# One ring of 1 MB slots for all operands, and 32-column TensorE tiles, in a two-problem attention decode kernel

## The chip, the cores and the metric

The kernel runs on one core of a Trainium2 chip. The metric is the device time of the launch in microseconds (us), as the median of several runs. The other figure used here, the span, goes from the first to the last instruction of one profiled run; it is about 2 us shorter. Each profile is of one run.

In the lines of the profile, PE is TensorE and PEld its weight loads, DVE is VectorE, ACT is ScalarE, POOL is GpSimd, and SPq is the queue of SyncE, which issues the loads. L337 is line 337 of the kernel. An arrow in brackets names what ended the idle time before an instruction. The granted clock is the share of TensorE's full clock that the chip allowed.

## The reference

Two independent problems, A and B, each do one decode step of grouped attention: one query row, 32 query heads, 16 key heads, 128 numbers per head. A looks at the last 2048 positions of its cache only, B at all 8192. The two output rows are joined.

```python
q = (x @ wq).reshape(32 heads, 128)          # x: 576 numbers, wq: 576 x 4096
scores = q . k * 128**-0.5                   # two query heads share one key head
o = softmax(scores) . v
out = o.reshape(4096) @ wo                   # wo: 4096 x 576
# A: k, v = last 2048 of 8192 positions;  B: k, v = all 8192 positions
```

All data are bf16. Every byte of K, V, wq and wo is read once: 102.8 MB. There is little arithmetic per byte, so the question is how well the kernel keeps its reads going.

## The kernel before

K and V come in slabs of 512 KB (2048 positions of one head, 4 KB per partition) through a ring of 13 slabs. wq and wo have their own region, in chunks. Each K slab is transposed on TensorE into PSUM, copied back to SBUF by ScalarE (half) and VectorE (half), and multiplied with a query matrix that is zero outside the two columns of the head:

```python
def pe_T(pe, s):                       # 16 transposes of a 512 KB slab of K
    ...
    ins = pe.matmul(pk_bf[bank][...], lhsT=slabs[:, b, t, :], rhs=ident[:, :], is_transpose=True, ...)

def pe_S(pe, s):                       # scores: 128 weight columns, of which 32 are heads
    for jj in range(4):
        ins = pe.matmul(sacc[:, jj * 512:(jj + 1) * 512], lhsT=qtm[:, P, g, :],
                        rhs=ktb[:, j, jj * 512:(jj + 1) * 512], start=(g == 0), stop=(g == HKV - 1))

def pe_V(pe, vi):                      # V is the weights, two columns of probabilities move
    for t in range(NBLK):              # NBLK = 16
        ins = pe.matmul(dst, lhsT=slabs[:, b, t, :], rhs=ptsb[P][:, bb, 2 * g:2 * g + 2], ...)
```

The order is: q of A, K of A, q of B, all of K of B (V of A is put in between), then all of V of B. wo of B is loaded before the V stage and applied during and after it.

## Time and profile before

The time is 292.9 us (291.66 to 293.63, three runs).

| What | Value | Where it is read |
|---|---|---|
| Span of the profiled run | 291.6 us | page header |
| Read from memory | 102.76 MB, 352 GB/s on average | DMA part of the page |
| Rate when the queue is never starved | 408 GB/s | windows, 220 to 270 us |
| Bytes at that rate | 252 us | 102.76 MB / 408 GB/s |
| Difference to the span | about 40 us | |

The page of the kernel before, the part with 40 equal slices of 7.29 us: the busy tenths of TensorE, its granted clock in tenths, the DMA engines' busy share in tenths, and the rate.

```profile
PE   0569995699999979997999989996395447445565
PEclk9999999985999999999999999999555555555555
DMA  5999999999999999999799998999879999999940
GB/s 162 317 327 409 354 351 352 371 398 401 406 406 398 410 409 380 355 356 389 295 301 368 375 375 297 379 405 412 318 267 412 408 409 406 409 407 408 407 161 2
```

The DMA engines look busy in nearly all slices, but only in the last quarter does the rate stay near 408 (slices 9 to 15 come close, with 398 to 410). The same kernel by windows (busy us of each engine and, in brackets, instructions; then the granted clock, the DMA share and the rate):

```profile
0.00:23.00 23.00, 10.32 (x162) 9.25 (x163) 0.00 (x0) 1.49 (x2) 6.13 (x11) 1.00 0.88 275
23.00:110.00 87.00, 77.42 (x952) 58.28 (x952) 31.20 (x51) 39.23 (x39) 0.00 (x0) 0.94 1.04 389
110.00:200.00 90.00, 84.94 (x1084) 61.98 (x1081) 37.67 (x53) 50.17 (x51) 0.00 (x0) 1.00 0.98 358
...
210.00:220.00 10.00, 7.04 (x222) 6.65 (x222) 5.14 (x23) 0.00 (x0) 0.00 (x0) 0.50 0.69 257
220.00:270.00 50.00, 26.92 (x903) 25.73 (x904) 6.03 (x38) 0.00 (x0) 0.00 (x0) 0.50 1.03 408
...
280.00:291.60 11.60, 6.08 (x196) 5.63 (x195) 2.45 (x14) 0.00 (x0) 0.00 (x0) 0.50 0.05 16
```

Taking in each window its length times (1 - rate / 408), the start loses 7.5 us, 23 to 110 us 4 us, the K stage of B (110 to 200 us) 11 us, the change to the V stage 4 us, and the end 11 us. Those are about 38 of the 40 us.

Why the K stage is slow is seen on the timeline of TensorE: a slab costs 16 transposes and four score matmuls back to back, here 119.46 - 118.56 = 0.90 us and 120.32 - 119.46 = 0.86 us. The columns are start, duration, engine, line, operation, output and inputs, shapes and count.

```profile
118.56 1.06 PE L337 MATMUL pk<-ident,slabs 128*128 128x128 bf16 x16
119.46 1.03 PE L356 MATMUL sacc<-ktb,qtm 128*128 128x512 bf16 x4
120.32 0.54 PE L479 MATMUL pk<-ptsb,slabs 128*128 128x2 bf16 x16
...
278.84 0.43 PE L479 MATMUL pk<-ptsb,slabs 128*128 128x2 bf16 x11
282.17 0.19 PE L479 MATMUL pk<-ptsb,slabs 128*128 128x2 bf16 x2 [2.90 <-issue]
```

About 1.76 us for 512 KB is 298 GB/s. With one V slab of A (0.40 us) after three of K, 2 MB take an estimated 5.7 us, or 369 GB/s, near the 358 of the stage. The last two lines are from the end: "2.90 <-issue" is idle time in which TensorE waited for nothing that the profile shows. Such gaps come about every 256 instructions in the V stage. Nearly all bytes have landed by 280 us (the last piece at 282.6 us), and TensorE has work until 289 us.

### The profile page before, as it was taken

The numbers are of one execution on the slowest core, as the hardware profiler recorded it, in microseconds if no ns is written. First come the engines' busy times: TensorE is split into PE (matmuls) and PEld (weight loads), VectorE is DVE, ScalarE is ACT, GpSimd is POOL, SyncE is SP. The second block draws the span as 40 slices with busy tenths as digits, with TensorE's granted clock in tenths as the row PEclk, the third lists the DMA queues.
The fourth block names the chain that finished last, engine by engine and source line by source line (L and its number), as shares of the span: only waits on it lengthen the run. The fifth ranks groups of instructions, "written<-read, shape, count | busy, mean of one in ns | idle before, by whom it ended". The sixth has DMA issues, their size and how long they took to land.

```text
span 291.6 us, 8755 instructions
## 1 busy us (share of the span) xinstructions
PE 224.6 (77%) x3930; PEld 178.9 (61%) x3930; DVE 87.8 (30%) x199; ACT 93.3 (32%) x94; POOL 6.1 (2%) x11
## 2 busy tenths in 40 slices
PE   0569995699999979997999989996395447445565
PEld 0568763489667757775677767775285437445554
DVE  0003331150344363336333363344541111011112
ACT  2004552221655557554655556553000000000000
POOL 8000000000000000000000000000000000000000
PEclk9999999985999999999999999999555555555555
DMA  5999999999999999999799998999879999999940
GB/s 162 317 327 409 354 351 352 371 398 401 406 406 398 410 409 380 355 356 389 295 301 368 375 375 297 379 405 412 318 267 412 408 409 406 409 407 408 407 161 2
DMA packets 37480, 103.33 MB, mean 354 GB/s; under 512 B 4162, under 2 KB 12356, under 8 KB 37444
## 3 DMA queue, kind: packets, MB, share of 16 engines
q1 hardware_dynamic: 37444, 102.78, 94.1%
q8 instruction: 31, 0.51, 0.7%
q14 instruction: 5, 0.04, 0.0%
HBM read 102.76 MB, written 0.00 MB: 352 GB/s over the span
## 4 chain that ended last, share of the span: by engine, by line
PE 51%; SPq 14%; DMA 12%; issue 12%; DVE 6%; ACT 4%; DVEq 0%; ACTq 0%
PE sacc L356 17%; PE pk L337 17%; DMA slabs<-in_B_v_cache_dram 7%; SPq L232 7%; DMA slabs<-in_A_k_cache_dram 5%; SPq L273 4%; PE sacc L479 4%; PE pk L479 4%; PE pk L310 3%; DVE ssb L394 3%; PE pk L493 3%; ACT psb L405 2%; SPq L230 2%; PE sacc L493 2%; ACT ktb L375 1%
## 5 line engine op out<-in xcount | busy, mean ns | idle before, releaser
L375 ACT ACTIVATE ktb<-pk 128x1024 bf16<-128x1024 bf16 x80 | 81.6, 1022 | 99.8 <-PE pk L337 99.8
L337 PE MATMUL pk<-ident,slabs 128*128 128x128 bf16 x1280 | 87.6, 222 | 8.6 <-DMA slabs<-in_A_k_cache_dram 7.1
L337 PEld LDWEIGHTS pk<-ident,slabs 128*128 128x128 bf16 x1280 | 78.5, 99 | 24.8 <-DMA slabs<-in_A_k_cache_dram 8.6
L356 PE MATMUL sacc<-ktb,qtm 128*128 128x512 bf16 x320 | 82.7, 381 | 4.3 <-DVE stat L394 4.3
L377 DVE COPY ktb<-pk 128x1024 bf16<-128x1024 bf16 x80 | 55.3, 691 | 97.8 <-PE pk L337 97.8
L356 PEld LDWEIGHTS sacc<-ktb,qtm 128*128 128x128 bf16 x320 | 28.0, 98 | 24.4 <-issue 5.3
L479 PE MATMUL sacc<-ptsb,slabs 128*128 128x2 bf16 x672 | 23.4, 165 | 13.0 <-issue 7.2
L310 PE MATMUL pk<-xsb,wreg 128*128 128x1 bf16 (+1 forms) x320 | 20.2, 172 | 12.7 <-DMA wreg<-in_A_wq_dram 12.7
L479 PEld LDWEIGHTS sacc<-ptsb,slabs 128*128 128x128 bf16 x672 | 21.0, 104 | 14.1 <-issue 8.5
L310 PEld LDWEIGHTS pk<-xsb,wreg 128*128 128x128 bf16 (+1 forms) x320 | 18.1, 104 | 14.9 <-issue 8.2
L479 PEld LDWEIGHTS pk<-ptsb,slabs 128*128 128x128 bf16 x608 | 20.0, 101 | 11.6 <-issue 5.4
L479 PE MATMUL pk<-ptsb,slabs 128*128 128x2 bf16 x608 | 21.4, 164 | 7.4 <-issue 5.2
L493 PE MATMUL pk<-ostage,wreg 128*128 128x1 bf16 x192 | 11.3, 165 | 5.7 <-issue 5.7
L493 PE MATMUL sacc<-ostage,wreg 128*128 128x1 bf16 x128 | 10.6, 165 | 5.7 <-issue 5.7
L493 PEld LDWEIGHTS pk<-ostage,wreg 128*128 128x128 bf16 x192 | 9.3, 104 | 8.8 <-issue 8.8
L394 DVE CUSTOM_DVE_ANT_0 ssb<-sacc,zrow 32x2048 bf16<-32x2048 f32 x5 | 11.4, 2279 | 1.8 <-PE sacc L356 1.8
L405 ACT ACTIVATE psb<-ssb,stat 32x2048 bf16<-32x2048 bf16 x5 | 9.9, 1988 | 3.8 <-DVE stat L399 3.8
L556 DVE CAST ostage<-sacc 128x2 bf16<-128x2 f32 x21 | 3.3, 159 | 25.8 <-PE sacc L479 25.8
L493 PEld LDWEIGHTS sacc<-ostage,wreg 128*128 128x128 bf16 x128 | 8.4, 104 | 2.9 <-issue 2.9
L323 DVE CAST qtm<-pk 128x32 bf16<-128x32 f32 x2 | 0.4, 192 | 30.3 <-PE pk L310 30.3
L556 DVE CAST ostage<-pk 128x2 bf16<-128x2 f32 x11 | 1.8, 159 | 14.7 <-PE pk L479 14.7
L493 PE MATMUL pk<-otsb,wreg 128*128 128x1 bf16 x128 | 4.2, 164 | 2.5 <-DVE stat L394 2.5
(49 smaller groups left out, 63.7 us busy)
## 6 DMA issues: line engine op xcount, KB each, us to landing
slabs<-in_B_k_cache_dram SPq DMA_DIRECT2D x64, 512.0 KB, 6.5
slabs<-in_B_v_cache_dram SPq DMA_DIRECT2D x64, 512.0 KB, 11.5
slabs<-in_A_k_cache_dram SPq DMA_DIRECT2D x16, 512.0 KB, 14.4
slabs<-in_A_v_cache_dram SPq DMA_DIRECT2D x16, 512.0 KB, 6.0
wreg<-in_A_wo_dram SPq DMA_DIRECT2D x4, 1152.0 KB, 12.9
wreg<-in_B_wo_dram SPq DMA_DIRECT2D x4, 1152.0 KB, 11.6
wreg<-in_A_wq_dram SPq DMA_DIRECT2D x4, 1024.0 KB, 8.7
wreg<-in_B_wq_dram SPq DMA_DIRECT2D x4, 1024.0 KB, 14.6
```

Source lines behind the costliest of these rows:

```text
L230: sp.dma_start(wqv[:, 0:4, cols], wq[0:512, cols].rearrange("(k p) n -> p k n", p=128)).then_inc(s_wq[P][c], 16)
L232: sp.dma_start(wqv[0:DM - 512, 4, cols], wq[512:DM, cols]).then_inc(s_wq[P][c], 16)
L273: sp.dma_start(slabs[:, b, :, :].rearrange("p t d -> p (t d)"), src).then_inc(s_slab_full[b], 16)
L310: ins = pe.matmul(pk[3][:, P * HQ + h:P * HQ + h + 1], lhsT=wqv[0:rows, kt, h * DH:(h + 1) * DH], rhs=xsb[0:rows, P, kt:kt + 1], start=(kt ...
L337: ins = pe.matmul(pk_bf[bank][:, (t - 8 * half) * 128:(t - 8 * half + 1) * 128], lhsT=slabs[:, b, t, :], rhs=ident[:, :], start=True, stop ...
L356: ins = pe.matmul(sacc[:, jj * 512:(jj + 1) * 512], lhsT=qtm[:, P, g, :], rhs=ktb[:, j, jj * 512:(jj + 1) * 512], start=(g == 0), stop=(g ...
L375: ins = eng.activation(dst, src, ACT.Copy)
L377: ins = eng.tensor_copy(dst, src)
L394: dve.tensor_tensor_reduce(out=ssb[P][0:HQ, c4 * SLAB:(c4 + 1) * SLAB], in0=sacc[0:HQ, :], in1=zrow[0:HQ, :], scale=1.0, scalar=-1.0e30, o ...
L405: act.activation(psb[P][0:HQ, c4 * SLAB:(c4 + 1) * SLAB], ssb[P][0:HQ, c4 * SLAB:(c4 + 1) * SLAB], ACT.Exp, bias=st(P, C_NB + c4), scale=S ...
L479: ins = pe.matmul(dst, lhsT=slabs[:, b, t, :], rhs=ptsb[P][:, bb, 2 * g:2 * g + 2], start=(t == 0), stop=(t == NBLK - 1))
L493: ins = pe.matmul(outT[P][nt], lhsT=wov[:, h, c0:c0 + 128], rhs=col, start=first, stop=last)
```

## The change

It is a rewrite. Its intent: let nothing but the reads take time.

- All of wq, K, V and wo go through one ring of 12 slots of 1 MB, 8 KB per partition, in the order of use. A K slot holds 4096 positions of one head of B, or 2048 of two heads of A.
- The scores and V use four column tiles of 32. Each tile has its own 32 weight columns and its own 32 output partitions, and the four are meant to run side by side. For V the roles are swapped: the probabilities are the weights, V moves.
- The softmax has 128 rows (four tiles of 32 heads), so its VectorE and ScalarE instructions run over rows a quarter as long.
- K of a chunk alternates with V of the chunk before. wo of B is loaded last.

The core of the diff, with cuts (here and below `...` marks what is left out):

```diff
-SLAB = 2048
-NBUF = 13
+SLOT = 4096
+NSLOT = 12
...
-            ins = pe.matmul(sacc[:, jj * 512:(jj + 1) * 512],
-                            lhsT=qtm[:, P, g, :],
-                            rhs=ktb[:, j, jj * 512:(jj + 1) * 512],
-                            start=(g == 0), stop=(g == HKV - 1))
+                for h in range(CW[P] // 512):
+                    for j in range(4):
+                        o = e * CH[P] + j * CW[P] + h * 512
+                        ins = pe.matmul(sacc[32 * j:32 * j + 32, h * 512:(h + 1) * 512],
+                                        lhsT=qtm[:, P, g * 32:(g + 1) * 32], rhs=kt[:, u, o:o + 512],
+                                        start=(g == 0), stop=(g == HKV - 1))
...
-            ins = pe.matmul(dst,
-                            lhsT=slabs[:, b, t, :],
-                            rhs=ptsb[P][:, bb, 2 * g:2 * g + 2],
-                            start=(t == 0), stop=(t == NBLK - 1))
+                for b in range(CB[P]):
+                    for j in range(4):
+                        t = e * NT[P] + j * CB[P] + b
+                        o = (b * 4 + j) * 512 + 30 * g + 30
+                        ins = pe.matmul(opsum[32 * j:32 * j + 32, 0:DH], lhsT=ptm[:, pb, o:o + 32],
+                                        rhs=slots[:, s, t * 128:(t + 1) * 128], ...)
...
+    def load_wq(P, k):
+        rows = 128 if k < 4 else DM - 512
+        return load(lambda: wqs[P][k * 128:k * 128 + rows, :], lambda v: v[0:rows, :], "wq")
...
+    pb1 = k_phase(1, 1, between_b1)      # K of the second chunk of B, V of the first in between
+    v_some(1, 0, vb0, HKV)
...
+    v_some(1, 1, vb1, HKV)
+    combine(1)
+    for k in range(5):
+        wo_part(1, k, load_wo(1, k))     # wo of B: last
```

## The prediction

> **What bounds it now.** The page's header: span 291.6 us, 102.8 MB moved, mean 352 GB/s. In the stretches where the queue is never starved (228 to 270 us, table of windows) the 16 DMA engines deliver 407 to 409 GB/s at a DMA share above 1.0. At 408 GB/s the bytes alone take 252 us, so about 40 us of the span is DMA time not used. I read four places in the slices and windows:
> - 0 to 23 us: 195 to 320 GB/s, with 4162 packets under 512 B (x, element by element) and 2 KB rows of wq.
> - 110 to 200 us, the K stage of B: 298 to 409 GB/s, mean about 358. The chain of waits shows it PE-bound: 16 transposes 0.89 us and four 512-column score matmuls 0.88 us, 1.77 us per 512 KB (296 GB/s). DMA issue waits 74.6 us for K evictions.
> - 208 to 217 us: ring full until the first V of B (257 GB/s), PE clock 0.50.
> - 280 to 291.6 us: no DMA. PE finishes V and wo at clock 0.50, with 2.8 us "issue" gaps about every 256 instructions.
>
> **What the change does.** The same bytes, in 1 MB slots (12 of them, 30 us of transfers at 408 GB/s), with long rows. Transposes stay: 32 x 56 ns = 1.8 us per K slot. Scores are 8 matmuls per slot on four column tiles: 8 x 220 ns = 1.76 us serial, 0.44 if four run at once. The Trainium skill, "TensorE: Matmul & The Clock Gate", Part 3, measures 2.38x for three column tiles, so I take 0.6 us. V now moves 128 columns against 32-column weights: 32 x 56 ns, 1.8 us serial, about 0.6 in fours. So K costs about 2.4 us and V 0.6 against 2.57 us of DMA each. Evictions per K slot: ACT 2 x 1.02 = 2.04 us, DVE 2 x 0.69 = 1.4; both fit. PE instructions fall from 7860 to about 6500 and spread evenly, so fetch gaps hide behind the ring. Added: the softmax weight chains (about 4 us of PE waiting each) and mode switches; 30 us of ring absorbs them. wo of B comes last, when V is done: only 16 small matmuls, one copy and the 1.5 us output write follow the last load.
>
> **Sum.** First bytes about 2 us; 102.8 MB at 408 GB/s 252; small dips (64-row wq slots, starts) 2; tail 4. That is 260 us, nearly all of it DMA. Even serial column tiles (K 3.6, V 1.8 us) would mostly hide: K plus V 5.4 us against 5.14.
>
> **Predicted: 260 us, 8 in 10 between 254 and 270.** Faster by over 2%: 0.96; within 2%: 0.03; slower: 0.01.
>
> **Signs.** DMA share of 9 in nearly all slices and 400 to 410 GB/s from about 3 us until 5 us before the end; chain of waits mostly DMA into slots; DMA issue waits on PE are just the ring's pace; score matmuls in fours, about 0.5 to 0.7 us per slot; last load to end under 5 us.
>
> **What would break it.** The PE clock. The half clock measured here doubles transposes (115 ns each at 23 us, before the clock rose). The same page, Part 4, says that transposes do not count as activity in the same way; scores, now four times shorter, may not hold the clock up. Then K takes about 4.7 us plus V 1.2, against 5.14: the ring runs dry of free slots in B's K stages, and the time goes to 275 to 285 us. Before, with idle gaps of 2.8 us between K slabs, the clock stayed at 1.0, so I give this one in ten. The other way: 8 KB rows could raise the rate to 415 GB/s, giving 255 us.

## The result

The time is 262.5 us (262.43 to 263.82, four runs) against 293.13 us for the kernel before. The ratio is 0.898, with a 95% interval of 0.895 to 0.901. Ratios here are worked out from the fast runs of both kernels, so they are not quite the ratio of the medians that are quoted.

The slices of the changed kernel (6.5 us each):

```profile
PE   0559995179899795778967649768665443443472
PEclk9999999658799799797999997797886755555555
DMA  7999999999999999999999999999999999999971
GB/s 263 420 328 409 409 417 419 233 421 414 418 414 410 421 413 414 416 420 416 424 420 419 419 420 421 419 420 420 421 422 415 425 421 419 422 417 421 423 325 55
```

TensorE is 66% busy, the DMA engines are busy from the first slice to the last but two, and the rate is 409 to 425 apart from the dips, mostly above 408. Two dips (slices 3 and 8) and the end stand out. By windows:

```profile
0.00:3.00 3.00, 0.00 (x0) 0.00 (x0) 0.00 (x0) 1.49 (x2) 2.24 (x14) 1.00 0.40 79
...
13.00:17.00 4.00, 1.97 (x16) 0.27 (x16) 0.00 (x0) 0.00 (x0) 4.00 (x3) 1.00 0.96 274
...
46.00:52.00 6.00, 1.05 (x8) 0.14 (x8) 0.00 (x0) 0.00 (x0) 0.00 (x0) 0.59 0.99 224
...
60.00:110.00 50.00, 41.56 (x753) 33.15 (x751) 19.99 (x36) 25.34 (x27) 0.00 (x0) 0.89 1.02 415
110.00:200.00 90.00, 64.94 (x1292) 52.28 (x1289) 31.28 (x53) 38.03 (x41) 0.00 (x0) 0.89 1.01 420
200.00:240.00 40.00, 18.36 (x548) 14.16 (x548) 0.76 (x4) 0.00 (x0) 0.00 (x0) 0.54 1.01 420
...
250.00:257.50 7.50, 3.96 (x116) 3.10 (x118) 0.05 (x1) 0.00 (x0) 0.00 (x0) 0.50 0.48 196
257.50:260.60 3.10, 0.65 (x16) 0.35 (x16) 0.31 (x1) 0.00 (x0) 0.00 (x0) 0.50 0.00 0
```

At 420 GB/s the bytes take 244.7 us. With the same sum as above, the start loses 2.4 us, the dips 1.4 and 2.8 us, 250 to 257.5 us 4.0 us, and the end without reads 3.1 us. The stage from 110 to 200 us, which had lost 11 us, loses nothing: TensorE is busy for 65 of 90 us and waits for data. The timeline of TensorE:

```profile
42.18 0.40 PE L298 MATMUL opsum<-slots,xpad 128*32 128x512 bf16 x4 [0.91 <-DVE xpad L285]
42.40 0.40 PE L298 MATMUL misc<-slots,xpad 128*32 128x512 bf16 x4
42.61 0.40 PE L298 MATMUL opsum<-slots,xpad 128*32 128x512 bf16 x4
...
54.93 6.47 PE L335 MATMUL ktps<-ident,slots 128*128 128x128 bf16 x64
61.33 0.62 PE L356 MATMUL sacc<-kt,qtm 128*32 128x512 bf16 x8
...
161.35 1.96 PE L335 MATMUL ktps<-ident,slots 128*128 128x128 bf16 x32 [0.51 <-DMA slots<-in_B_k_cache_dram]
163.24 0.61 PE L356 MATMUL sacc<-kt,qtm 128*32 128x512 bf16 x8
163.84 0.63 PE L448 MATMUL opsum<-slots,ptm 128*32 128x128 bf16 x32
```

Four matmuls of 512 columns on four tiles start every 0.22 us (42.18, 42.40, 42.61), which is what one such matmul took before (0.88 us for four). So the four tiles do run side by side. Between transposes, eight take about 0.55 to 0.6 us instead of 1.76; why the gain is smaller there was not tested. The Trainium skill ("TensorE: Matmul & The Clock Gate", Part 3) has 2.38 times for three column tiles; this trace shows 4 times for four in an unbroken stream and about 3 times in the K slots.

The end, on the timeline of all engines: the last load releases 16 small matmuls, a copy and the output write.

```profile
257.48 0.67 PE L483 MATMUL misc<-slots,opj 128*32 128x144 bf16 x16 [0.36 <-DMA slots<-in_B_wo_dram]
258.21 0.31 DVE L489 CAST outsb<-misc 128x144 bf16<-128x144 f32 x1 [8.15 <-PE misc L483]
258.54 0.64 SPq L494 DMA_DIRECT2D out_dram<-outsb  x1
```

### The profile page after: what moved, and what is told of

Read it like the earlier page. It is cut to its first block, busy times and chain, and to the rows that moved or that the text cites. A ratio compares the mean times of both kernels' runs of the same rounds, so it can differ in the third digit from the quotient of the medians.

```text
span 260.6 us, 7123 instructions
## 1 busy us (share of the span) xinstructions
PE 171.7 (66%) x3292; PEld 132.6 (51%) x3292; DVE 68.9 (26%) x126; ACT 85.2 (33%) x92; POOL 21.6 (8%) x31
## 2 busy tenths in 40 slices
DMA packets 16369, 103.22 MB, mean 396 GB/s; under 512 B 1618, under 2 KB 1620, under 8 KB 6996
## 3 DMA queue, kind: packets, MB, share of 16 engines
HBM read 102.76 MB, written 0.00 MB: 394 GB/s over the span
## 4 chain that ended last, share of the span: by engine, by line
DMA 56%; SPq 27%; PE 14%; issue 1%; DVE 1%; ACT 0%
SPq L244 27%; DMA slots<-in_B_v_cache_dram 21%; DMA slots<-in_B_k_cache_dram 10%; DMA slots<-in_B_wo_dram 10%; PE ktps L335 10%; DMA slots<-in_B_wq_dram 9%; DMA slots<-in_A_k_cache_dram 6%; PE sacc L356 2%; PE opsum L448 1%; PE misc L483 0%; DVE qrow L307 0%; PE opsum L298 0%; SPq L105 0%; PE misc L298 0%; DVE srow L411 0%
## 5 line engine op out<-in xcount | busy, mean ns | idle before, releaser
L335 PE MATMUL ktps<-ident,slots 128*128 128x128 bf16 x1280 | 94.0, 243 | 24.6 <-DMA slots<-in_B_k_cache_dram 24.2
L335 PEld LDWEIGHTS ktps<-ident,slots 128*128 128x128 bf16 x1280 | 87.6, 111 | 32.7 <-DMA slots<-in_B_k_cache_dram 28.4
L342 ACT ACTIVATE kt<-ktps 128x1024 bf16<-128x1024 bf16 x80 | 78.7, 1022 | 74.9 <-PE ktps L335 74.8
L345 DVE COPY kt<-ktps 128x1024 bf16<-128x1024 bf16 x80 | 55.4, 692 | 93.0 <-PE ktps L335 93.0
L448 PE MATMUL opsum<-slots,ptm 128*32 128x128 bf16 x1280 | 31.7, 256 | 26.6 <-DMA slots<-in_B_v_cache_dram 26.5
L448 PEld LDWEIGHTS opsum<-slots,ptm 128*32 128x32 bf16 x1280 | 24.5, 114 | 39.7 <-DMA slots<-in_B_v_cache_dram 35.1
L356 PE MATMUL sacc<-kt,qtm 128*32 128x512 bf16 x320 | 25.4, 395 | 0.7 <-DVE kt L345 0.7
L220 POOL MEMSET ptm<- 128x8192 uint32 x2 | 13.8, 6924 | 0.0
L483 PE MATMUL misc<-slots,opj 128*32 128x144 bf16 x256 | 8.4, 307 | 5.4 <-DMA slots<-in_B_wo_dram 3.3
L483 PEld LDWEIGHTS misc<-slots,opj 128*32 128x32 bf16 x256 | 6.6, 134 | 6.9 <-DMA slots<-in_B_wo_dram 4.2
```

The costliest lines, as they stand in the source:

```text
L220: add("pool", lambda pool, b=b: pool.memset(ptm[:, b, :].bitcast(U32), 0), writes=[("ptm", b)])
L335: ins = pe.matmul(ktps_bf[q][:, t * 128:(t + 1) * 128], lhsT=slots[:, s, (8 * q + t) * 128:(8 * q + t + 1) * 128], rhs=ident[:, :], start= ...
L342: add("act", lambda act, q=q, dst=dst: act.activation(dst, ktps_bf[q], ACT.Copy), reads=[("bank", q)], writes=[("kt", u, q)])
L345: add("dve", lambda dve, q=q, dst=dst: dve.tensor_copy(dst, ktps_bf[q]), reads=[("bank", q)], writes=[("kt", u, q)])
L356: ins = pe.matmul(sacc[32 * j:32 * j + 32, h * 512:(h + 1) * 512], lhsT=qtm[:, P, g * 32:(g + 1) * 32], rhs=kt[:, u, o:o + 512], start=(g ...
L448: ins = pe.matmul(opsum[32 * j:32 * j + 32, 0:DH], lhsT=ptm[:, pb, o:o + 32], rhs=slots[:, s, t * 128:(t + 1) * 128], start=(g == 0 and b ...
```

## The experiments

The theory: after the change the reads bound the kernel nearly everywhere, their rate is set by the row length, and TensorE has slack. The rivals are that the time still comes from how TensorE's work is arranged (side-by-side tiles, alternation, ring depth), and that the dips and the end have other causes. Eleven kernels ran, the kernel before beside them, and all gave correct results. The changed kernel itself ran before these. Differences to its 262.5 us therefore are good to 1 or 2 us, and smaller ones say nothing. Where the ratio to the kernel before gives another size, both are told.

### Undoing single parts: row length

```diff
-                return a[0, i, r0:r0 + n, :].rearrange("(p t) d -> p (t d)", p=128)
+                return a[0, i, r0:r0 + n, :].rearrange("(h p t) d -> p h (t d)", h=2, p=128)
```

> Changed kernel, with one edit: each 1 MB slot of K and V of B is read as 2 x 4 KB per partition instead of 8 KB; number of transfers, ring and engine work stay. Theory A (bytes per row set the rate; one 4 KB packet took 159 ns before, one of 8 KB takes 312 ns): the rate in the V stage falls from 420 to about 409 GB/s and the time rises by 4 to 5 us, to 267. Rival B (the rate rose because there are half as many transfers, or because the engines disturb memory less): rate 418 to 421 and time within 0.7 us of 262.5.

Measured: 267.62 us (266.95 to 267.74), ratio to before 0.908 (0.903 to 0.914). The window of the V stage, which showed 420 GB/s in the changed kernel, with rows of 4 KB:

```profile
200.00:240.00 40.00, 18.24 (x496) 13.78 (x500) 1.98 (x12) 0.30 (x1) 0.00 (x0) 0.50 1.02 409
```

The medians differ by 5.1 us, the ratios to the kernel before (0.908 and 0.898) by about 3 us, and the rate falls back to that of the kernel before. The 67.1 MB of K and V of B at 409 instead of 420 GB/s are an estimated 4.3 us. The number of transfers, the ring and the engines' work are the same. So rows of 8 KB instead of 4 KB give 420 instead of 408 to 409 GB/s, and theory A holds. In the trace a row of 4 KB takes 159 to 162 ns on its DMA engine, one of 8 KB 312 ns.

### Undoing single parts: the order of the tiles

```diff
-                for b in range(CB[P]):
-                    for j in range(4):
+                for j in range(4):
+                    for b in range(CB[P]):
```

(and the same turn of the two loops of the scores)

> Changed kernel, with the loops turned so that successive matmuls of the scores and of V use the same column tile (V: eight in a row), so that little runs side by side. Theory A (transfers bound the kernel; the column tiles only had to bring TensorE under the transfer time): V per slot rises from 0.45-0.6 to about 1.7 us and scores from 0.54 to about 1.1 us at full clock, the clock stays up more, TensorE waits less for DMA, and the time stays within 2 us of 262.5. Rival B (side-by-side tiles are what the time comes from): K plus V over 5 us, ring starved, time above 268 us.

Measured: 263.32 us (262.82 to 264.09), ratio 0.894 (0.889 to 0.900). V per slot, on the timeline of TensorE at full clock:

```profile
163.83 1.34 PE L448 MATMUL opsum<-slots,ptm 128*32 128x128 bf16 x32
```

V costs 1.34 us instead of 0.63; the scores did not get slower (0.62 us), perhaps because they have only two matmuls per tile. So the edit took less of the overlap away than expected, and on that point the expectation missed. Still, V at twice the cost left the time where it was: 0.8 us more by the medians, while the ratio of 0.894 is even below 0.898.

### Adding TensorE work

```diff
-                for t in range(8):
+                for t in list(range(8)) * 2:     # every transpose of K twice
```

> Changed kernel with every K transpose done twice (same result), about 1.8 us more of TensorE per K slot at full clock: K 4.3 us and V 0.6 instead of 2.5 and 0.6, near the 5.4 us per pair that the prediction gave for column tiles that do not overlap. Theory A (prediction: such an excess mostly hides behind the ring and the V slots): time at most 270 us. Rival B (without side-by-side tiles the K stages are bound by TensorE): stages of K alone and of 2 K to 1 V run at under 350 GB/s and the time is 275 us or more.

Measured: fast runs of 267.57 and 270.31 us; two more, 271.84 and 271.68, are marked slow as they lie over 1.5% above the fastest. Their clocks (0.94 and 0.92) are those of the fast runs (0.95 and 0.92), so this may be the kernel's own spread. The ratio of the fast runs is 0.916 (0.908 to 0.923). The window from 110 to 200 us:

```profile
110.00:200.00 90.00, 86.00 (x1787) 77.11 (x1785) 27.76 (x41) 38.70 (x39) 0.00 (x0) 1.00 0.99 402
```

With 64 transposes per slot (3.7 us), an estimated 40 x 1.8 = 72 us of TensorE work was added, and 5 to 8 us of it show in the fast runs. The rate was 413 GB/s from 20 to 43 us and 402 from 110 to 200 us; the lowest slice there has 313. The fast runs lie on both sides of the 270 us of theory A, the median of all four is 271.0, and none reaches the 275 us of the rival. TensorE thus has much slack, but not without limit. In the stage with one V to each K, a pair took 4.7 us of TensorE (153.33 to 158.01 us), still less than the 5.0 us of its two transfers.

### Undoing single parts: alternation and ring depth

```diff
-        if i >= 2:
-            v_some(1, 0, vb0, 1)          # e6: no V between the K slots of the last K stage
```

> Changed kernel without the alternation in the last K stage: all 16 K slots of B's second chunk, then all 16 V slots of its first. Theory A (a K slot alone costs TensorE 2.5 to 2.56 us against 2.5 us of transfer, and the ring takes up the rest): within 1 us of 262.5, TensorE 90% or more busy in that K stage. Rival B (alternation is needed to keep the queue fed): the rate falls clearly below 410 GB/s in that stage and the time rises by 3 us or more.

```diff
-NSLOT = 12
+NSLOT = 6                                 # e5
```

> Changed kernel with a ring of 6 slots (6 MB, 15 us of transfers) instead of 12; the kernel before had 6.5 MB. Theory A (TensorE keeps pace per slot, so the ring only has to cover short waits): within 1 us of 262.5. Rival B (the deep ring is what hides the softmax chains and cold stretches): DMA rate dips in B's K stages and the time rises by 4 us or more.

Measured: without alternation 263.2 us (262.73 to 264.36), with TensorE busy for 39.4 of the 42 us of that K stage and 420 GB/s. With 6 slots 263.76 us (262.84 to 264.48), 416 instead of 420 GB/s from 110 to 200 us, with two slices below 400 (387 and 392). The first agrees with its theory A. The second is 1.3 us slower by the medians, a little more than the 1 us that was allowed, and far from the 4 us of its rival; the ratios (0.897 and 0.899, against 0.898) show no difference for either. Neither alternation nor the depth of the ring explains the gain; once a K slot costs TensorE no more than its transfer takes, 6 MB of lookahead is nearly enough.

### Undoing single parts: what is loaded last

```diff
-    v_some(1, 1, vb1, HKV)
+    v_some(1, 1, vb1, HKV - 6)
+    wob = [load_wo(1, k) for k in range(5)]
+    v_some(1, 1, vb1, HKV)                # the last six V slots land after wo
     combine(1)
```

> Changed kernel, but wo of B is loaded ahead of the last six V slots, so that V lands last. Theory A (loading wo last hides the combination of V and the 128 wo matmuls under its own transfers): after the last load TensorE still has one V slot (1.0 us), the combination (about 3 us) and 128 wo matmuls (about 4 us at half clock), so the end comes about 7 us later: 268 to 270 us. Rival B (the order of the last loads does not matter, as the end is set by the slowest DMA engine): within 1 us of 262.5.

Measured: 269.71 us (269.17 to 270.64), ratio 0.916 (0.910 to 0.922). The timeline of the end:

```profile
256.61 1.04 PE L448 MATMUL opsum<-slots,ptm 128*32 128x128 bf16 x32 [1.41 <-DMA slots<-in_B_v_cache_dram]
...
258.57 1.92 PE L470 MATMUL misc<-acc,pick 128*128 128x32 f32 x8 [0.92 <-DVE acc L464]
...
260.86 4.03 PE L483 MATMUL misc<-slots,opj 128*32 128x144 bf16 x128 [0.38 <-DVE opj L474]
...
265.28 0.64 SPq L494 DMA_DIRECT2D out_dram<-outsb  x1
```

From the last load to the output write 8.7 us pass, against 1.1 us (257.48 to 258.54) in the changed kernel. The order of the last loads is worth 7 us (5 us by the ratios).

### One part of the change alone, on the kernel before

```diff
-            ins = pe.matmul(sacc[:, jj * 512:(jj + 1) * 512],
-                            lhsT=qtm[:, P, g, :],
+            ins = pe.matmul(sacc[32 * jj:32 * jj + 32, jj * 512:(jj + 1) * 512],
+                            lhsT=qtm[:, P, g, 0:32],
...
-        dve.tensor_tensor_reduce(...)      # copy of the scores and their maximum in one
+        # four copies of 512 columns to partitions 0 to 31, then tensor_reduce for the maximum
```

> The kernel before, with one part of the change alone: its score matmuls go to four column tiles of 32 (the maximum is then taken in a copy and a reduction). Theory A (B's K stage was bound by TensorE at 1.77 us per 512 KB, half of it scores): scores per slab fall from 0.88 to about 0.3 us, the stage runs at 400 GB/s or more instead of 358, and the time falls by 8 to 11 us, to 282 to 285. Rival B (the stage was bound by evictions or by the ring): within 2 us of before. Neither removes the V stage's end at half clock, so 270 or less would refute both.

Measured: 286.23 us (284.3 to 287.49) against 293.93, ratio 0.973 (0.968 to 0.979). The timeline of TensorE in the K stage, and then the window of the stage:

```profile
120.95 1.14 PE L337 MATMUL pk<-ident,slabs 128*128 128x128 bf16 x16
122.03 0.40 PE L356 MATMUL sacc<-ktb,qtm 128*32 128x512 bf16 x4
122.36 1.14 PE L337 MATMUL pk<-ident,slabs 128*128 128x128 bf16 x16
```

```profile
110.00:200.00 90.00, 77.04 (x1253) 57.76 (x1251) 47.54 (x70) 52.70 (x52) 0.00 (x0) 0.88 1.00 380
```

A slab now costs 122.36 - 120.95 = 1.41 us instead of 1.76: the scores take 0.33 us instead of 0.86, but the 16 transposes between them 1.08 instead of 0.90. The stage runs at 380 GB/s instead of 358, less than the 400 that was expected. The gain of 7.7 us is just under the lower end of theory A and refutes its rival. So the score tiles alone give about a quarter of the 31 us; the stage of the kernel before was bound by TensorE. What still held it below 400 was not tested. The trace shows three candidates: the slower transposes; at the end of each chunk the separate maximum (2.29 us), which stands in the chain of waits; and the clock, which averages 0.88 in the stage (1.00 before).

### The two dips

The dips coincide with the last slot of wq of A and of B: 64 rows, which went to 64 of the 128 partitions. The experiment sends these rows as 128 half rows. x then needs two columns for them, one with zeros in the odd places and one with zeros in the even places.

```diff
-        rows = 128 if k < 4 else DM - 512
-        return load(lambda: wqs[P][k * 128:k * 128 + rows, :], lambda v: v[0:rows, :], "wq")
+        if k < 4:
+            return load(lambda: wqs[P][k * 128:k * 128 + 128, :], lambda v: v, "wq")
+        return load(lambda: wqs[P][512:DM, :].rearrange("r (h n) -> (r h) n", h=2),
+                    lambda v: v[:, 0:2048], "wq")
...
+                    kk, o = (k, n * 512) if k < 4 else (4 + j // 2, (n % 4) * 512)
```

> Changed kernel, with one edit: the last 64 rows of wq go as 128 half rows to all 128 partitions instead of 64 whole rows to 64 partitions. Theory A (the two dips to 160-310 GB/s at 13-16 us and 46-52 us come from writing only half of the partitions): both dips go, about 1.4 + 2.8 us are gained, 258 to 259 us. Rival B (the dips come from something else at that time, such as the stalled TensorE, its low clock, or the GpSimd memsets): the dips stay and the time stays at 262.5 us within 0.5.

Measured: 258.44 us (258.38 to 258.50), ratio to before 0.877 (0.871 to 0.884). The same two windows as above:

```profile
13.00:17.00 4.00, 0.00 (x0) 0.00 (x0) 4.00 (x2) 0.00 (x0) 4.00 (x1) 1.00 1.03 419
46.00:52.00 6.00, 5.00 (x68) 2.76 (x68) 1.00 (x3) 1.01 (x2) 0.00 (x0) 0.72 1.02 426
```

Both dips are gone and 4.1 us are gained (6 us by the ratios), as theory A has it. The Trainium skill ("SBUF — State Buffer", Door 1: The DMA port swizzle) says that partitions 0 to 63 reach only half of the 16 DMA ports, with 196 GB/s measured for 1 MiB; in the dips of the changed kernel single microseconds show 160 to 307 GB/s and the longer dip 224 on average, which roughly agrees.

The 4.00 us of VectorE from 13 to 17 us in this kernel are no work: the copies of 64 numbers that spread x were issued while GpSimd cleared a large tile, and took 11.05 us instead of 0.18.

```profile
3.39 13.79 POOL L222 MEMSET ptm<- 128x8192 uint32 x2
...
7.09 11.09 DVE L283 COPY xz<-xrow 1x64 bf16<-1x64 bf16 x2 [7.09 <-DMA xrow<-in_A_x_dram]
```

It put TensorE's first matmul off from 7.4 to 18.3 us, and the rate did not suffer: twelve slots give 30 us. The same skill page (SBUF: two separate sides) calls the port pair that GpSimd and VectorE share an exclusive lock, which the one that starts first holds for its whole instruction. The trace agrees that the copy is blocked and not slowed in proportion, but the wait outlasted one instruction: the first clearing ended at 10.32 us, and the copies only at 18.14 and 18.17 us, after a second one and four short ones that followed it without a pause (to 18.08 us).

### The slow last stretch

From 250 to 257.5 us the rate falls although reads are still queued. The trace has 16 completions for each load, one for the part of each DMA engine (it does not name the engines). Here they are for the first, a middle and the last load of e1 (the middle one completed at about 102 us), in us after the earliest engine, and for the last load of the two kernels that follow (worked out from the trace, one number per engine, sorted):

```
e1, first load      0.0 0.1 0.1 0.2 0.3 0.3 0.3 0.3 0.4 0.4 0.4 0.4 0.5 0.5 0.6 0.6
e1, middle load     0.0 0.1 0.1 0.2 0.4 0.5 1.2 1.3 1.6 1.8 1.8 1.9 1.9 2.1 2.1 3.5
e1, last load       0.0 0.0 0.2 0.4 0.5 0.7 1.2 1.3 4.7 4.8 4.9 5.0 5.0 5.1 5.1 6.4
e9, last load       0.0 0.3 0.4 0.4 0.5 1.1 1.2 1.3 4.8 5.0 5.0 5.0 5.0 5.0 5.0 5.2
e8, last load       0.0 0.1 0.1 0.2 0.3 0.4 0.8 1.1 4.4 4.5 4.8 4.9 6.2 6.3 6.3 6.3
```

Eight engines fall behind in steps, mostly of 1.3 to 1.4 us, one engine per step, and do not catch up in the rest of the run. In the same trace there are 26 fetches of instructions of 16 KB, nearly all of 1.0 to 1.1 us on a DMA engine. TensorE has 6643 instructions there, which is 26 pieces of 256 (e9: 6387 and 25 fetches; e8: 8203 and 32). The steps follow the fetches: those at 29.7 and 36.6 us, for example, are followed by the first late engine in the load that completes from 31.8 us on, and a second in the one from 36.9 us. Two experiments on top of e1 change the number of fetches.

```diff
+            for _ in range(30 if (P, c) == (1, 1) else 0):      # and in each wo slot
+                pe.matmul(sacc[0:1, 0:1], lhsT=ident[:, 0:1], rhs=ident[:, 0:1], start=True, stop=True)
```

> The kernel of e1_wq128 plus 30 idle matmuls of one column in each of the last 26 slots: 780 matmuls, 1560 TensorE instructions, about 6 more instruction fetches of 16 KB. In the trace of e1 each fetch sets one of eight DMA engines back by 1.3 us, in turn, for good, and the last engine ends 6.4 us after the first. Theory A (these set-backs fix the end): 32 fetches, all eight at 5 to 6.5 us or more, and the time is within 1 us of 258.4 or up to 1.4 us longer, with the spread of the last load at 6.4 us or more and more engines in the late group. Rival B (the spread comes from something else): same number of late engines as in e1 (8, one of them at 6.4).

```diff
-OUTW = DM // 4
+OUTW = DM // 2
...
-                for j in range(4):
+                for j in range(2):
...
-                    ins = pe.matmul(misc[32 * j:32 * j + 32, 0:OUTW], lhsT=opj[:, P, jj:jj + 32],
+                    ins = pe.matmul(misc[64 * j:64 * j + 64, 0:OUTW], lhsT=opj[:, P, jj:jj + 64],
```

> The kernel of e1_wq128, and wo on two column tiles of 64 instead of four of 32: 128 matmuls and 256 TensorE instructions fewer, one fetch of 16 KB. Theory A (each fetch sets one of eight DMA engines back 1.3 us for good): the fetch that came at 246 us in e1 comes later or not at all before the loads end, the spread of the last load falls from 6.4 to about 5.1 us, 257 to 257.6 us. Rival B: no change of the spread, 258.4 us, or a little more for the longer end.

Measured for e9: 257.31 us (257.22 to 257.43), ratio to before 0.876 (0.872 to 0.880), spread of the last load 5.2 us instead of 6.4, as theory A has it. It is the fastest kernel. It ran in another call than e1, so the 1.1 us between them are not from one chip; the evidence is the spread.

Measured for e8: 270.06 us (269.82 to 270.26), a miss: 1.4 us at most were expected, and it took 11.6 us more than e1. The loads ended as early as in e1, with four engines at 6.2 to 6.3 us instead of one at 6.4, so on the spread theory A is borne out. But TensorE no longer kept up at half clock, because of gaps of the kind that the kernel before had in its V stage:

```profile
215.37 0.27 PE L459 MATMUL opsum<-slots,ptm 128*32 128x128 bf16 x1
218.31 0.58 PE L459 MATMUL opsum<-slots,ptm 128*32 128x128 bf16 x13 [2.67 <-issue]
...
253.84 0.40 PE L459 MATMUL opsum<-slots,ptm 128*32 128x128 bf16 x6 [0.77 <-issue]
```

With 124 instead of 64 instructions per V slot, 256 instructions pass in about 3.3 us, and then TensorE stands for 2.7 us, until the next piece is there: the fetch in this gap began at 215.8 us and took 1.0 us. The six long gaps of the kernel before likewise each hold the start of a fetch, at 247.9, 254.1, 260.4, 266.9, 273.4 and 279.6 us. When the loads are done, the gap shrinks: 0.77 us at 253.84 us in e8, 0.27 us at 285.93 us in the kernel before. So e8 produced the end of the kernel before on purpose, and few instructions per byte matter while the DMA engines are full.

A last attempt was to give the last load to eight engines only (the code is shortened).

```diff
+            for m in (0, 2, 1, 3):           # r in 0..3: 16 transfers of 8 partitions, 4 apart
+                p0 = 32 * m + r
+                sp.dma_start(slots[p0:p0 + 29:4, s, 0:(hi - lo) * DM], src[p0:p0 + 29:4, lo * DM:hi * DM])
```

> As e9_wo64, and the last 576 KB of wo go as 16 transfers of 8 partitions each; the Trainium skill (DMA: Bandwidth & Descriptors) says that such a transfer uses the eight lowest-numbered engines alone. If the eight engines that the fetches set back are the other eight, the end comes 1 to 1.4 us earlier than in e9; if they are these eight, 1.4 to 2.8 us later. No change would say that the transfer is not confined to eight engines.

Measured: 261.28 us (261.04 to 261.63), 4.0 us more than e9. The direction is that of "these eight" in the expectation, but the size lies above its 1.4 to 2.8 us. The trace shows why: each of the 16 small transfers has eight completions after the one at its issue, so it was confined to eight engines, and of these six are early and two late (the last transfer: six from 249.7 to 251.1 us, two at 255.1 us; the load before: eight from 245.7 to 246.8, eight from 251.6 to 252.0 us). So the eight are neither the set-back ones nor the others, but a mixture, which the expectation did not foresee. The two late engines, now with twice their share, end 3.0 us after the last completion of e9 (252.1 us), which is most of the 4.0 us.

## Why the prediction was right

The prediction was 260 us (254 to 270), the measurement 262.5 us. Point by point:

- **The reads bound the kernel after the change.** Right: 60 to 250 us run at 415 to 423 GB/s with TensorE waiting, and doubling the cost of V (e3) or leaving out the alternation (e6) moves the time by less than calls differ.
- **The four places of the kernel before.** Right as a place for each loss. For the K stage the score tiles alone gained 7.7 us (b1). For the end, V loaded last costs 7 us (e4), and more instructions per slot bring the "issue" gaps back (e8). Which part of the rewrite mended the start, and which the change to the V stage, was not tested alone.
- **The costs of K and V.** K 2.4 us: measured 1.89 + 0.6 = about 2.5 us. V 0.6 us: measured 0.63 us at full and 1.04 us at half clock.
- **The rate of 408 GB/s.** This term was mis-sized. It gave 252 us, and 420 GB/s give 244.7, 7.3 us less. The prediction named 8 KB rows as a possible gain and left them out of the sum; e2 shows 3 to 5 us of it for K and V of B alone.
- **Small dips, 2 us.** Mis-sized: 1.4 + 2.8 us, for the 64-row slots alone (e1).
- **Tail, 4 us.** The end after the last load is 3.1 us, but the stretch before it, in which some DMA engines have finished and others have not, loses another 4.0 us. It is not in the prediction. The claim that "fetch gaps hide behind the ring" came out right for TensorE by another way: the gaps hardly occur at the lower pace of instructions (the longest "issue" wait is 1.0 us), whereas in e8 they occurred and a ring of 12 did not hide them. It also leaves out that each fetch takes its 1.3 us from one DMA engine.
- The too low rate and the missing terms nearly cancel: 244.7 + 2.4 + 4.2 + 4.0 + 3.1 = 258.4 of the 260.6 us of the span. Of the rest, about 1.2 us are the rate of 411 to 416 GB/s outside the dips between 17 and 110 us, and 1.1 us the 0.45 MB that were moved beyond the 102.76 (103.22 MB in all, mostly fetched instructions). The time is about 2 us more than the span, which the sum left out too. That the number came within 2.5 us is therefore partly luck; the mechanism, reads as the bound, is not.
- **"Even serial column tiles would mostly hide".** Borne out in kind by e7, where 72 us of added TensorE work cost 5 to 8 us. But e7's K and V pair stays under its transfer time (4.7 against 5.0 us), where the prediction had 5.4 against 5.14, and serial tiles were not run, so the claim itself is not shown.
- **The risk of the half clock.** It came about only in short spells: between 67 and 197 us the clock fell to 0.50 eight times, for 3.4 us each, and the 32 transposes at 156.30 us took 3.54 us instead of 1.96, while the rate stayed at 415 to 420 GB/s. The average clock of 0.81 holds these spells and the V stage (0.54 from 200 to 240 us). At the start of B's K stage the clock rose with nothing but transposes running.

## What to carry to other kernels

When reads bound a kernel, look at their rate and not at the DMA busy share: rows of 8 KB, all 128 partitions in every load, and no late work behind the last load were worth about 4, 4 and 7 us here (e2, e1, e4), with the DMA share at 0.9 or more nearly throughout. Bring each engine under the transfer time per piece; beyond that, deeper rings and finer alternation gave little here (e5, e6). Count instructions per byte as well: here their fetches went through the same DMA engines, held TensorE up for 2.7 us each where they came too fast (e8), and left single engines 1.3 us behind for the rest of the run (e1).

## What the Trainium skill lacked or had wrong

- "TensorE: Matmul & The Clock Gate", Part 4, says that transposes do not count as activity for the clock in the same way, and that the full clock does not engage for them. In the changed kernel only transposes ran from 54.93 to 61.33 us, and the granted clock rose from 0.50 to 1.00 within that time (0.50 from 59 to 60 us, 0.66 from 60 to 61 us, 1.00 from 61 us).
- "DMA: Bandwidth & Descriptors", Where 436 GB/s comes from, gives a ceiling of 435 GB/s, and a later section (iDMA fabric) has 408.7 for 4 KiB rows, which agrees with the 408 to 409 here. No page has the next step: 8 KB rows ran at 420 GB/s, against 409 with 4 KB rows in an otherwise equal kernel (e2).
- "Runtime: NRT & Kernel Launch", Instruction fetch mechanics, calls the cost of a 16 KB boundary mostly hidden. With full DMA queues the gap was 2.7 to 2.9 us per 256 short instructions (kernel before, e8), and 0.3 to 0.8 us once the loads were done. Each fetch set one of eight DMA engines back by 1.3 us for the rest of the run (e1); no page has the latter.
- "TensorE: Matmul & The Clock Gate", Part 3, has three column tiles of 512 columns (2.38 times). Four ran in 0.22 us, 4 times, in an unbroken stream; eight between transposes took 0.55 to 0.6 us, about 3 times.
